# Token blocks 2 and 3 of an adaLN kernel's first part: rows turned by VectorE and a DRAM scratch in place of TensorE transposes

## The chip, the cores and the metric

The kernel runs on one NeuronCore of a Trainium2 chip. The metric is the device time of one execution in microseconds (us). Before the change the median of three runs is 2213.26 us (2213.18 to 2213.31).

A core has five engines with a queue each, and each queue runs in order: TensorE (PE, matmuls and transposes into PSUM), VectorE (DVE), ScalarE (ACT), GpSimd (POOL) and SyncE (SP), which here issues the DMAs. An instruction waits on semaphores at the head of its queue, and all behind it on that engine waits too.

## The reference

One transformer block with adaptive layer norm, on 2048 tokens of width 576, all in float32. Cut to what matters:

```python
mod = (silu(c) @ w_mod).reshape(1, 6, 1, 576)
sa, ca, ga, sb, cb, gb = (mod[:, j] for j in range(6))
h = layernorm(x) * (1 + ca) + sa
x = x + ga * A(h)          # 32 query heads of width 18, one shared key and value head:
                           #   q = h @ wq;  k = h @ wk;  v = h @ wv
                           #   softmax(q k^T / sqrt(18)) v, then @ wo
h = layernorm(x) * (1 + cb) + sb
x = x + gb * B(h)          # layernorm, @ w1 + b1, gelu, @ w2 + b2 (width 4608)
```

The change is in the first lines: from `x` to the transposed, modulated `h` that the projections to q, k and v read.

## The kernel before

The kernel has three parts: projections (to about 129 us), attention, and the channel MLP. Only the first is touched.

The 2048 tokens are four blocks (`tb` 0 to 3) of 512, a block being four tiles (`t`) of 128 tokens. The projections contract over the 576 channels, so `h` is needed with channels on partitions: five chunks (`k` 0 to 4) of 128 channels by 512 tokens, the last with 64 channels held twice. For each block this happens:

- `ln1_stats(tb, t)`: VectorE's bn_stats and bn_aggr and three small GpSimd operations give a tile's scale `rs` and offset `nb`.
- `ln1_apply(tb, t, e)`: the tile is normalised from `XT` into the row buffer `Z1` (L192 on ScalarE, L194 on VectorE): 576 columns, and the last 64 once more.
- `h_chunk(tb, zt, k)`: four 128x128 transposes on TensorE (`tr`, L157) turn a chunk into one PSUM slot of `psB`, of which there are three. Then `h_evac`: ScalarE applies the modulation (L230, into `hf`) and rounds to fp32r (L234, into the buffer `big`), and GpSimd or VectorE takes what the rounding lost (L235).
- `q_chunk(tb, m, zt, mid, n)`: a product. `proj` makes 14 matmuls (L250) into a `psB` slot, ScalarE copies it out twice (L280, L281), GpSimd takes the difference (L282), and SP stores both to the scratch `qscr` in DRAM (L286).

A block has five products, m = 4, 0, 1, 2, 3 at the steps i = 0 to 4 of the loop. In the middle of a product stands a "part": four score matmuls of 512 columns (L321), two for each of the two PSUM slots `psA`, and two VectorE reductions (L346 in `smax_part`) that find the maxima and free the slots.

The order on every engine is the order of the code. The main loop runs over `tb` and the steps, and after the product of a step it places the work for later blocks: chunks of block `tb + 1`, and by the tables `NAPPLY` and `NSTAT` normalisations and statistics of the blocks after. The third and fourth tile of block 2 are normalised at step 0 of block 1 (the first two at step 4 of block 0), those of block 3 at steps 3 and 4 of block 1. The chunks of the next block stand at

```python
for k in {1: (0, 1, 2), 2: (3, 4)}.get(i, ()) if tb else {3: (0, 1, 2), 4: (3, 4)}.get(i, ()):
    h_chunk(tb + 1, nz, k)
```

so in blocks 1 and 2 three chunks follow the product of step 1 and two that of step 2.

Of the kernel before, what the change touches and what calls it, by code (L numbers as in the profile page):

```python
# [8 lines left out]
F32 = mybir.dt.float32  # L9
# [5 lines left out]
S, D, H, DH, F = 2048, 576, 32, 18, 4608  # L15
NB = 4
TB = S // NB
NT = TB // 128
KD = 5
# [13 lines left out]
def block_kernel(ctx: ExitStack, tc, x, wqkv, wo, w1, b1, w2, b2, c, wmod, ident_in, out):  # L33
    nc = tc.nc
    ve, ac, po, pe, sy = nc.vector, nc.scalar, nc.gpsimd, nc.tensor, nc.sync

    per = ctx.enter_context(tc.tile_pool(name="per", bufs=1))
    dr = ctx.enter_context(tc.tile_pool(name="dr", bufs=1, space=bass.MemoryType.DRAM))
# [14 lines left out]
    def psB(): return PS["t"].tile([128, 512], F32, name="psB", bufs=PS["b"])  # L53
# [3 lines left out]
    def big(): return per.tile([128, 10, 512], F32R, name="big", bufs=3)  # L57
# [10 lines left out]
    w2sum = dr.tile([NG, 128, 4, 2, 288], F32, name="w2sum")  # L68
    turned = [dr.tile([D, 128], F32, name="turned%d" % n) for n in range(2)]
    turned0 = dr.tile([D, 128], F32, name="turnedA")  # L70
    qscr = dr.tile([NB, 2, H * DH, TB], F32, name="qscr")


# [15 lines left out]
    p1 = ph1.__enter__()  # L89
# [66 lines left out]
    def tr(o, Z, k):  # L156
        pe.transpose(o, Z[:, 128 * k:128 * (k + 1)], ident)  # L157
# [14 lines left out]
    Zs = {}  # L172
# [3 lines left out]
    def ln1_stats(tb, t):  # L176
        X = XT[:, NT * tb + t, :]
        mv = p1.tile([128, 2], F32, name="mv1", bufs=4)
        rs = p1.tile([128, 1], F32, name="rs1", bufs=12)
        nb = p1.tile([128, 1], F32, name="nb1", bufs=12)  # L180
        ln_stats2(X, ln_stats1(X), mv, rs, nb)
        RN[tb, t] = (rs, nb)

    def ln1_apply(tb, t, e):
        if t == 0:
            Zs[tb] = p1.tile([128, NT, 640], F32, name="Z1")
        Z = Zs[tb]
        X = XT[:, NT * tb + t, :]
        rs, nb = RN.pop((tb, t))
        for o, i in ((Z[:, t, :D], X), (Z[:, t, D:], X[:, 512:])):  # L190
            if e is ac:
                ac.activation(o, i, AF.Identity, scale=rs, bias=nb)  # L192
            else:
                ve.tensor_scalar(o, i, rs, nb, op0=ALU.mult, op1=ALU.add)  # L194

    mcol = p1.tile([128, 2, KD], F32, name="mcol")

# [29 lines left out]
    def h_evac(p, zt, k, e, first=False):  # L227

        hf = p1.tile([128, TB], F32, name="hf", bufs=3)
        ac.activation(hf, p, AF.Identity, scale=mcol[:, 1, k:k + 1], bias=mcol[:, 0, k:k + 1])  # L230
        if first:
            ve.tensor_copy(zt[:, k, :], hf)
        else:
            ac.activation(zt[:, k, :], hf, AF.Copy)  # L234
        e.tensor_tensor(zt[:, KD + k, :], hf, zt[:, k, :].bitcast(F32), op=ALU.subtract)  # L235

    def h_chunk(tb, zt, k):
        p = psB()
        for t in range(NT):
            tr(p[:, 128 * t:128 * (t + 1)], Zs[tb][:, t, :], k)  # L240
        h_evac(p, zt, k, ve if tb == 1 and k in (1, 3, 4) else po, tb == 1 and k < 3)

    def proj(o, wh, wl, c0, c1, zt, mid=None, n=0):
# [28 lines left out]
    def q_chunk(tb, m, zt, mid, n):  # L272

        w = 126 if m < KD - 1 else 128
        wd = 126 if m < KD - 1 else 72
        pq = psB()
        proj(pq[:w], wqh, wql, 126 * m, 126 * m + w, zt, mid, n)
        qs = p1.tile([128, 2, TB], F32R, name="qs", bufs=2)
        qf = p1.tile([128, TB], F32, name="qf", bufs=2)
        ac.activation(qf[:w], pq[:w], AF.Copy)  # L280
        ac.activation(qs[:w, 0], pq[:w], AF.Copy)  # L281
        po.tensor_tensor(qs[:w, 1], qf[:w], qs[:w, 0].bitcast(F32), op=ALU.subtract)  # L282
        if m == KD - 1:
            if tb >= 2:
                key_diff(tb, qf)
        sy.dma_start(qscr[tb, :, 126 * m:126 * m + wd, :].rearrange("s p t -> p s t"), qs[:wd].bitcast(F32))  # L286
        return qf, qs

    def k_block(tb, qs):

        pk = psB()
        for i in range(2):
            pe.matmul(pk, pick[:, i, :], qs[:, i, :], start=(i == 0), stop=(i == 1))
        ac.activation(KS[:, TB * tb:TB * (tb + 1)], pk, AF.Identity, bias=ones)

    def v_block(tb, qf):
        pk = psB()
        for i in range(NT):
            pe.transpose(pk[:, 128 * i:128 * (i + 1)], qf[:, 128 * i:128 * (i + 1)], ident)
        ve.tensor_copy(V[:, NT * tb:NT * (tb + 1), :DH],  # L300
                       pk.rearrange("p (i c) -> p i c", i=NT)[:, :, 72:72 + DH])
# [6 lines left out]
    def load_q(n):  # L308
        tb, qd = divmod(n, NQ)
        if n not in QST:  # L310
            new_q(n)
        q = QST[n]
        for g in range(2):
            for r in range(3):
                src = qscr[tb, r // 2, 4 * DH * qd:4 * DH * (qd + 1), :]
                src = src.rearrange("(p g d) t -> g d p t", p=2, g=2)[g]
                sy.dma_start(q[64 * g + DH * r:64 * g + DH * (r + 1)].bitcast(F32), src)
# [30 lines left out]
    def smax_fin1(n):  # L348
        m = MR[n] = pa.tile([128, 16], F32, name="mxf", bufs=2)
        mm = MX.pop(n)  # L350
        if n == 0:
            ve.tensor_reduce(m, mm, axis=AX.X, op=ALU.max)
        else:
            ve.tensor_reduce(m[:, :8], mm[:, :8, :], axis=AX.X, op=ALU.max)
            ve.tensor_reduce(m[:, 8:], mm[:, 8:, :3], axis=AX.X, op=ALU.max)
# [14 lines left out]
    for t in range(NT):  # L370
        ln1_stats(0, t)
        if t:
            ln1_apply(0, t - 1, ve if t % 2 else ac)
    ln1_apply(0, NT - 1, ac)
    pick = p1.tile([128, 2, 128], F32R, name="pick")
    ones = p1.tile([128, 1], F32, name="ones")
# [28 lines left out]
    def dense(n, w, x):  # L405

        p = psB()
        for _ in range(n):
            pe.matmul(p, w, x, start=True, stop=True)
# [35 lines left out]
    def unit():  # L445
        nonlocal u1
        smax_half(1, u1 % 2, u1 // 2)
        u1 += 1
# [5 lines left out]
    for tb in range(NB):  # L454
        nz = big() if tb + 1 < NB else None
        for i, m in enumerate((4, 0, 1, 2, 3)):
            np_ = NPART[tb][i]
            if i == 2:
                parts.extend((u, tb) for u in range(8))
            mid = {(NB - 1, 1): unit, (NB - 1, 4): lambda: last.popleft()()}.get((tb, i), part)  # L460
            qf, qs = q_chunk(tb, m, zt, mid, np_ + 1 if np_ else 0)
            if i == 0:
                qv = qf, qs
            if i == 1:
                k_block(tb, qv[1])
                v_block(tb, qv[0])
                if tb == 0:
                    load_q(0)
            if i == 2:
                if tb == 0:  # L470
                    load_q(1)
            if tb == NB - 1:
                if i == 0:
                    unit()
                elif i == 3:
                    smax_fin1(0)
                if i == 4:
                    dense(5, wqh[:, 0, :128], KS[:, :512])
                    unit()
                    dense(4, wqh[:, 0, :128], KS[:, :512])  # L480
            if nz is not None:
                for k in {1: (0, 1, 2), 2: (3, 4)}.get(i, ()) if tb else {3: (0, 1, 2), 4: (3, 4)}.get(i, ()):
                    h_chunk(tb + 1, nz, k)
            if tb < 2:
                for _ in range(NAPPLY[tb][i]):
                    b, t = applies.popleft()
                    ln1_apply(b, t, ve if b == 1 and t % 2 else ac)
                for _ in range(NSTAT[tb][i]):
                    ln1_stats(*stats.popleft())
        zt = nz  # L490
# [521 lines left out]
    for n in range(NQT):  # L1012
# [8 lines left out]
        for tok in order:  # L1021
            if tok[0] == "V":
                g = int(tok[1:])
                while g:
                    i = min(g, 4 - pq % 4)
# [16 lines left out]
            elif tok == "WP":  # L1042
                h2 = part.popleft()
                p = psB()
# [495 lines left out]
```

## Time and profile before

| | |
|---|---|
| median of three runs | 2213.26 us |
| the profiled execution's own time | 2214.96 us |
| its span, first to last instruction | 2212.9 us |
| mean granted TensorE clock | 0.998 |
| block 1 of the first part (its products) | about 48.0 to 72.7 us |
| block 2 | about 72.7 to 97.6 us |
| TensorE transposes of the rows of blocks 2 and 3 | 40, at 56.6 to 88.4 us |

Times in the text are microseconds from the span's start. A timeline row has start, length, engine, line, operation, output <- inputs, shape and count, and in brackets how long the engine sat idle before it and what released it. A row that merges several instructions gives the length of the whole group. An engine's next instruction can start before the last one's row ends, since they overlap a little.

### The profile page before, as it was taken

What the parts mean: (1) busy time and instruction counts of PE and PEld (TensorE: products, weight loads), DVE (VectorE), ACT (ScalarE), POOL (GpSimd) and SP (SyncE); (2) the same over time, 40 slices, a digit from 0 to 9 for tenths busy, and PEclk for the clock granted to TensorE, in tenths of its full rate; (3) what the DMA queues carried; (4) which work ended last, traced back from release to release, by engine and by line L of the source; (5) the groups of instructions that cost most, each with busy time, mean ns of one, the idle gap of its engine ahead of it and who ended that gap; (6) DMA issues with size and microseconds to landing.
All of it is one profiled execution on the core that took longest, in us unless ns stands there. A gap on an engine that the chain in (4) does not pass through costs nothing.

```text
span 2212.9 us, 46091 instructions
## 1 busy us (share of the span) xinstructions
PE 2193.5 (99%) x16559; PEld 1441.7 (65%) x16559; DVE 1935.3 (87%) x3421; ACT 1626.0 (73%) x3114; POOL 1520.2 (69%) x1760
## 2 busy tenths in 40 slices
PE   8999999999999999999999999999999999999999
PEld 6654445454544445444454445898988899889898
DVE  7589999999999999999999992888888878787887
ACT  5569999999999999999999998544445444343443
POOL 7654356667777677678675640888899767877776
PEclk9999999999999999999999999999999999999999
DMA  6232143333433443443343321666767746676664
GB/s 228 88 134 93 34 132 119 132 128 114 138 124 128 127 138 103 126 141 117 122 128 124 125 71 59 200 195 190 201 186 202 208 131 179 184 217 189 178 183 124
DMA packets 233528, 317.67 MB, mean 144 GB/s; under 512 B 58351, under 2 KB 124287, under 8 KB 233301
## 3 DMA queue, kind: packets, MB, share of 16 engines
q1 hardware_dynamic: 233157, 314.59, 46.4%
q8 instruction: 131, 2.15, 0.4%
q14 instruction: 96, 0.79, 0.1%
q10 hardware_dynamic: 144, 0.15, 0.0%
HBM read 205.92 MB, written 98.51 MB: 138 GB/s over the span
## 4 chain that ended last, share of the span: by engine, by line
PE 93%; DVE 1%; ACT 1%; issue 0%; ACTq 0%; DVEq 0%
PE psC L952 24%; PE psB L1176 18%; PE psA L1279 16%; PE psB L962 14%; PE psM L321 13%; PE psB L751 2%; PE psB L972 2%; PE psA L1313 1%; PE psA L751 1%; PE psB L250 0%; PE psB L359 0%; PE psM L962 0%; ACT P L964 0%; DVE mx L346 0%; DVE gs L1188 0%; ACT h L1185 0%
## 5 line engine op out<-in xcount | busy, mean ns | idle before, releaser
L964 ACT ACTIVATE P<-psB 128x512 f32<-128x512 f32 x2013 | 1055.6, 621 | 49.0 <-PE psM L321 24.4
L984 DVE TENSOR_REDUCE mx<-psM 128x1 f32<-128x512 f32 x1476 | 930.5, 681 | 27.6 <-PE psM L321 12.9
L962 PE MATMUL psB<-qst,KS 64*128 64x512 f32 x2013 | 604.8, 434 | 0.1
L321 PE MATMUL psM<-KS,qst 64*128 64x512 f32 x1722 | 594.0, 435 | 0.7 <-DVE mx L339 0.3
L952 PE MATMUL psC<-P,V 128*32 128x256 f32 (+3 forms) x6608 | 569.0, 440 | 0.0
L962 PEld LDWEIGHTS psB<-qst,KS 64*128 64x128 f32 x2013 | 302.1, 184 | 215.7 <-ACT P L964 184.6
L321 PEld LDWEIGHTS psM<-KS,qst 64*128 64x128 f32 x1722 | 285.4, 184 | 190.1 <-DVE mx L984 140.9
L1176 PE MATMUL psB<-ops,w1a 128*128 128x512 f32 x1512 | 393.9, 396 | 0.2 <-DVE h L1191 0.2
L1176 PEld LDWEIGHTS psB<-ops,w1a 128*128 128x128 f32 x1512 | 270.1, 188 | 46.8 <-DVE h L1191 0.6
L952 PEld LDWEIGHTS psC<-P,V 128*32 128x32 f32 x6608 | 147.1, 108 | 188.5 <-issue 160.9
L1285 DVE TENSOR_TENSOR XT<-psA,XT 128x576 f32<-128x576 f32 x330 | 241.2, 751 | 16.4 <-PE psA L1279 11.0
L1279 PEld LDWEIGHTS psA<-w2s,big 128*128 128x128 f32 x1584 | 223.6, 188 | 12.1 <-DVE XT L1285 0.2
L1279 PE MATMUL psA<-w2s,big 128*128 128x288 f32 x1584 | 230.1, 294 | 0.0
L1253 POOL TENSOR_TENSOR big<-s,big 128x512 fp32r<-128x512 f32 x132 | 170.9, 1295 | 10.6
L982 DVE CUSTOM_DVE_ANT_0 xc<-psM,xc 128x512 f32<-128x512 f32 x246 | 165.6, 680 | 11.8 <-PE psM L321 4.5
L1185 ACT ACTIVATE h<-psB,b1t 128x512 f32<-128x512 f32 x144 | 97.9, 680 | 105.7 <-PE psB L1176 99.3
L1189 ACT ACTIVATE psB<-gs 128x512 f32<-128x512 f32 x144 | 86.7, 602 | 119.9 <-DVE gs L1188 119.9
L975 ACT ACTIVATE xc<-psB 128x512 f32<-128x512 f32 x246 | 154.3, 627 | 5.5 <-PE psM L321 1.9
L788 POOL TENSOR_TENSOR os<-O,os 128x512 fp32r<-128x512 f32 x31 | 39.8, 1285 | 169.6 <-ACT os L787 169.5
L1188 DVE SCALAR_TENSOR_TENSOR gs<-psB,h 128x512 f32<-128x512 f32 x144 | 98.7, 686 | 38.7 <-ACT psB L1186 38.6
L822 POOL TENSOR_TENSOR r<-r,r 128x256 fp32r<-128x256 f32 (+1 forms) x162 | 121.8, 752 | 13.0
L1194 ACT ACTIVATE big<-h 128x512 fp32r<-128x512 f32 x39 | 24.7, 634 | 139.5 <-DVE h L1191 139.5
(215 smaller groups left out, 3289.2 us busy)
## 6 DMA issues: line engine op xcount, KB each, us to landing
w1a<-w1scr SPq DMA_DIRECT2D x252, 256.0 KB
w2s<-w2sum SPq DMA_DIRECT2D x132, 288.0 KB
w1scr<-r SPq DMA_DIRECT2D x126, 256.0 KB
w2s<-w2scr SPq DMA_DIRECT2D x76, 288.0 KB
w2scr<-r SPq DMA_DIRECT2D x72, 288.0 KB
w2sum<-r SPq DMA_DIRECT2D x72, 288.0 KB
qst<-qscr SPq DMA_DIRECT2D x192, 72.0 KB
w1a<-w2scr SPq DMA_DIRECT2D x33, 288.0 KB
```

The source lines that it names most:

```text
L321: pe.matmul(o, QST[n][64 * g:64 * g + 64, p, 128 * qt:128 * (qt + 1)], KS[64 * g:64 * g + 64, 512 * kb:512 * (kb + 1)], start=True, stop=True)
L822: po.tensor_tensor(o[:, n:2 * n], src, o[:, :n].bitcast(F32), op=ALU.subtract)
L952: pe.matmul(PVt[n][32 * j:32 * (j + 1), cs], V[:, kc, :], t[:, j, cs], start=(kc == 0 and h0 == 0), stop=(kc == 15), skip_group_check=True)
L962: pe.matmul(t, KS[64 * g:64 * g + 64, 128 * kc:128 * (kc + 1)], QST[n][64 * g:64 * g + 64, i, :], start=True, stop=True)
L964: ac.activation(P[n, kc][:, 2 * i + g, :], t, AF.Exp, scale=SCALE)
L975: ac.activation(XC[-1], t, AF.Relu)
L982: ve.tensor_tensor_reduce(c, t, c, 1.0, -3.0e38, ALU.add, ALU.max, o)
L984: ve.tensor_reduce(o, t, axis=AX.X, op=ALU.max)
L1176: pe.matmul(o, x, y, start=(first and i == 0), stop=(i == len(terms) - 1), skip_group_check=True)
L1253: po.tensor_tensor(unit(u, 1), x, unit(u, 0).bitcast(F32), op=ALU.subtract)
L1279: pe.matmul(p[:, i, :288], x[:, ts_], W2S[k][:, y], start=(bool(first) and q == 0), stop=(q == 2), skip_group_check=True)
L1285: ve.tensor_tensor(o, p[:, :, :288], o, op=ALU.add)
```

## The change

For blocks 2 and 3 the rows are no longer turned by TensorE. `ln1_apply` leaves out the second copy of the last 64 columns and lets VectorE transpose the tile in place; that transpose works within squares of 32 by 32. After every second tile SP writes the two tiles to a scratch `hscr` in DRAM (channels by tokens), eight DMAs of 32 partitions by 18 by 32 elements. A new function `h_load` reads the scratch back into the same row buffer, seen as five chunks of 512 tokens. ScalarE then reads a chunk there instead of in PSUM. `Z1` has two buffers instead of one. `h_load` stands at step 1 of the block, and the chunks move from steps 1 and 2 to 2 and 3. Blocks 0 and 1 keep TensorE's transposes.

```diff
+    hscr = [dr.tile([D, TB], F32, name="hscr%d" % n) for n in range(2)]
...
-            Zs[tb] = p1.tile([128, NT, 640], F32, name="Z1")
+            Zs[tb] = p1.tile([128, NT, 640], F32, name="Z1", bufs=2)
...
-        for o, i in ((Z[:, t, :D], X), (Z[:, t, D:], X[:, 512:])):
+        for o, i in ((Z[:, t, :D], X), (Z[:, t, D:], X[:, 512:]))[:1 if tb > 1 else 2]:
...
+        if tb > 1:
+            ve.transpose(Z[:, t, :D], Z[:, t, :D])
+            if t % 2:
+                for p in range(0, 128, 32):
+                    for i in (t - 1, t):
+                        sy.dma_start(hscr[tb % 2][:, 128 * i + p:128 * i + p + 32].rearrange("(c f) n -> f c n", f=32),
+                                     Z[p:p + 32, i, :D].rearrange("f (c n) -> f c n", n=32))
+
+    def h_rows(tb):
+
+        return Zs[tb].rearrange("p t c -> p (t c)").rearrange("p (k n) -> p k n", n=TB)
+
+    def h_load(tb):
+
+        H, scr = h_rows(tb), hscr[tb % 2]
+        sy.dma_start(H[:, :KD - 1], scr[:512].rearrange("(k p) n -> p k n", p=128))
+        for q in range(2):
+            sy.dma_start(H[64 * q:64 * q + 64, KD - 1], scr[512:])
...
     def h_chunk(tb, zt, k):
-        p = psB()
-        for t in range(NT):
-            tr(p[:, 128 * t:128 * (t + 1)], Zs[tb][:, t, :], k)
+        if tb > 1:
+            p = h_rows(tb)[:, k]
+        else:
+            p = psB()
+            for t in range(NT):
+                tr(p[:, 128 * t:128 * (t + 1)], Zs[tb][:, t, :], k)
...
-                for k in {1: (0, 1, 2), 2: (3, 4)}.get(i, ()) if tb else {3: (0, 1, 2), 4: (3, 4)}.get(i, ()):
+                if tb and i == 1:
+                    h_load(tb + 1)
+                for k in {2: (0, 1, 2), 3: (3, 4)}.get(i, ()) if tb else {3: (0, 1, 2), 4: (3, 4)}.get(i, ()):
                     h_chunk(tb + 1, nz, k)
```

How the instructions stand now, on three engines. Line numbers of the changed kernel lie about 20 higher: L249 is the old L230, L302 and L303 the old L280 and L281, L308 the old L286, L368 the old L346.

ScalarE in block 1, before: the key copy of step 1 (`KS`) and behind it the chunks of block 2 (`hf` from a PSUM slot, `big` from `hf`).

```order
L294 ACTIVATE KS_83<-psB_662,ones_194 128x512
L230 ACTIVATE hf_677<-psB_672,mcol_140 128x512
L234 ACTIVATE big_588<-hf_677 128x512
L230 ACTIVATE hf_686<-psB_681,mcol_140 128x512
L234 ACTIVATE big_588<-hf_686 128x512
```

The same place now (`Z1_585` is the row buffer of block 2, `Z1_791` that of block 3).

```order
L316 ACTIVATE KS_85<-psB_680,ones_196 128x512
L302 ACTIVATE qf_727<-psB_703 126x512
L303 ACTIVATE qs_726<-psB_703 126x512
L249 ACTIVATE hf_732<-Z1_585,mcol_142 128x512
L253 ACTIVATE big_598<-hf_732 128x512
```

The first chunk has moved behind the copies of the product of step 2, and reads the loaded row buffer. The normalisations of block 3 (`Z1_791`) follow the fifth chunk, as before.

VectorE across steps 3 and 4 of block 1 in the changed kernel (before, the same rows without the transpose).

```order
L368 TENSOR_REDUCE mx4_610<-psA_762 128x2
L368 TENSOR_REDUCE mx4_610<-psA_766 128x2
L197 STREAM_TRANSPOSE Z1_791<-Z1_791 128x576 x2
L146 BN_STATS bst_807<-XT_74 128x6
L150 BN_STATS bst_807<-XT_74 128x6
L151 BN_AGGR mv1_804<-bst_807 128x2
L368 TENSOR_REDUCE mx4_610<-psA_822 128x2
```

Two transposes of block 3's rows now stand between the reductions of step 3 and those of step 4.

SP's queue from step 3 of block 0 to step 2 of block 1, before: only stores of products to `qscr`.

```order
L286 DMA qscr_71<-qs_491 126x2x512
L286 DMA qscr_71<-qs_559 126x2x512
L286 DMA qscr_71<-qs_613 72x2x512
L286 DMA qscr_71<-qs_656 126x2x512
L286 DMA qscr_71<-qs_732 126x2x512
```

And now.

```order
L308 DMA qscr_73<-qs_493 126x2x512
L308 DMA qscr_73<-qs_561 126x2x512
L201 DMA hscr0_71<-Z1_585 32x18x32 x8
L308 DMA qscr_73<-qs_623 72x2x512
L201 DMA hscr0_71<-Z1_585 32x18x32 x8
L308 DMA qscr_73<-qs_674 126x2x512
L211 DMA Z1_585<-hscr0_71 128x4x512
L213 DMA Z1_585<-hscr0_71 64x512 x2
L308 DMA qscr_73<-qs_726 126x2x512
```

Two groups of eight writes and the load of three DMAs have come in between the stores.

## The prediction

> **What bounds the kernel now.** I read the page first: the busy shares and the chain that ended last.
>
> ```profile
> span 2212.9 us, 46091 instructions
> PE 2193.5 (99%) x16559; PEld 1441.7 (65%) x16559; DVE 1935.3 (87%) x3421; ACT 1626.0 (73%) x3114; POOL 1520.2 (69%) x1760
> PE 93%; DVE 1%; ACT 1%; issue 0%; ACTq 0%; DVEq 0%
> ```
>
> TensorE (PE) is busy 99% of the span and holds 93% of the chain. A microsecond taken from TensorE in its dense stretches is a microsecond of the total, and so is one of new idleness. The change lies in the first 130 us, so next comes the table by stretches, for block 1 (48.0 to 72.7 us) and block 2 (72.7 to 97.6 us). Its columns after the length are the busy times of PE, PEld, DVE, ACT and POOL, the granted clock, the DMA share and GB/s.
>
> ```profile
> 48.00:72.70 24.70, 24.01 (x117) 16.82 (x116) 16.91 (x25) 20.19 (x35) 20.09 (x29) 1.00 0.31 105
> 72.70:97.60 24.90, 23.76 (x115) 16.00 (x113) 12.53 (x12) 14.35 (x25) 13.49 (x11) 1.00 0.28 93
> ```
>
> TensorE binds in both. But in block 1, ScalarE (ACT) is busy 20.2 of 24.7 us and VectorE (DVE) 16.9: an engine that gets new work, or a new wait at the head of its queue, has 5 to 8 us to lose before TensorE feels it.
>
> **What is removed.** The timeline of PE has the transposes (L157) and what stands around them.
>
> ```profile
> 56.57 1.53 PE L157 MATMUL psB<-ident,Z 128*128 128x128 f32 x12 [0.33 <-DVE V L300]
> ...
> 62.30 1.03 PE L157 MATMUL psB<-ident,Z 128*128 128x128 f32 x8
> 63.70 1.90 PE L250 MATMUL psB<-big,wA 128*126 128x512 f32 x7 [0.36 <-ACT qs L281]
> ...
> 73.72 0.73 PE L321 MATMUL psA<-KS,qst 64*128 64x512 f32 x4
> ...
> 87.33 1.04 PE L157 MATMUL psB<-ident,Z 128*128 128x128 f32 x8
> 88.73 1.89 PE L250 MATMUL psB<-big,wA 128*126 128x512 f32 x7 [0.36 <-ACT qs L281]
> ...
> 109.99 1.41 PE L250 MATMUL psB<-big,wA 128*126 128x512 f32 x5 [0.33 <-ACT qs L281]
> ```
>
> In block 1's stretch (rows for block 2) the twelve cost 1.53 us. The eight cost 1.40 (63.70 - 62.30; in block 2's stretch 88.73 - 87.33), their slot wait of 0.36 included: without them the next product takes another of the three psB slots, one long free. The 0.33 ahead of the twelve stays: block 3, which makes no transposes, has it at the same place (109.99). So 2.93 a stretch, **5.9 us** for two, if nothing else comes late.
>
> **What is added, and where it queues.** VectorE gets eight transposes of 128x576, and each pair of tiles is written to DRAM by eight DMAs ("puts") in pieces of 32 floats. No first-part row has these, but the second part makes the same ones. The first row below is VectorE's; the next two are SP's timeline of four puts each; then two stretches with the DMA's share and GB/s last; then the stretch and the SP wait that price a 2 KB-row transfer.
>
> ```profile
> L615 DVE STREAM_TRANSPOSE Z<-Z x8: 767/768/769, 577.6 to 1126.1; 128x576 f32<-128x576 f32 x8
> 1126.88 2.00 SPq L618 DMA_DIRECT2D turnedA<-Z  x4
> 1472.69 2.21 SPq L694 DMA_DIRECT2D turned<-BC  x4
> 1128.00:1130.00 2.00, 2.00 (x16) 0.71 (x16) 1.97 (x7) 1.69 (x5) 1.78 (x3) 1.00 0.73 126
> 1130.00:1132.00 2.00, 2.00 (x17) 0.63 (x17) 1.86 (x5) 2.00 (x5) 1.85 (x3) 1.00 0.02 4
> 35.00:36.00 1.00, 1.00 (x6) 0.79 (x5) 0.97 (x4) 0.96 (x2) 0.33 (x2) 1.00 0.88 285
> SPq L317 <- DMA qscr<-qs: 6.1, 2, 3.3
> ```
>
> A put holds SP for 0.50 to 0.55 us and the DMA engines for 0.58 (73.7 KB at 126 GB/s); the last lands at most 1.1 us after its issue, since the DMA is quiet from 1130. A q store of 516 KB takes 1.8 us at 285 GB/s, yet the next SP instruction waits 3.3 us for its landing, so 1.5 us are fixed.
>
> Now block 2, whose rows are made in block 1. The next rows are ScalarE's and SP's timelines there.
>
> ```profile
> 49.74 2.28 ACT L192 ACTIVATE Z<-XT,nb,rs 128x576 f32<-128x576 f32 x4
> ...
> 62.56 0.60 ACT L280 ACTIVATE qf<-psB 126x512 f32<-126x512 f32 x1 [1.19 <-PE psB L250]
> 63.05 0.59 ACT L281 ACTIVATE qs<-psB 126x512 fp32r<-126x512 f32 x1
> 63.53 0.78 ACT L230 ACTIVATE hf<-psB,mcol 128x512 f32<-128x512 f32 x1
> 64.34 0.64 ACT L234 ACTIVATE big<-hf 128x512 fp32r<-128x512 f32 x1
> 64.88 0.76 ACT L230 ACTIVATE hf<-psB,mcol 128x512 f32<-128x512 f32 x1
> 52.95 0.31 SPq L286 DMA_DIRECT2D qscr<-qs  x1
> ```
>
> 1. *SP.* The rows of tiles 0 and 1 are normalised from 49.74 and turned by 52.2, but their puts stand behind the store of 52.95, free at 53.3. Eight puts at 0.53: 57.5. A store: 57.8. Eight puts of tiles 2 and 3: 62.0. A store: 62.4. Then the load, which waits for the last put.
> 2. *Landing of the puts.* SP alone would give 63.1 (62.0 + 1.1). The DMA engines have from about 53.8 sixteen puts at 0.58 and a 295 KB store (1.0 us): 64.1, and some 0.5 for the landing: **64.6**.
> 3. *The load.* Its first DMA moves 1.05 MB in 2 KB rows: 3.7 us at 285 GB/s, or 2.7 at 389 (a stretch further down), and 1.5 fixed: 4.2 to 5.2. I take 5.0, near the store's rate: **69.6**.
> 4. *ScalarE.* Its first chunk of block 2 now stands behind the copies of block 1's third product (62.56), where before the fourth chunk stood (63.53). Twelve transposes less and the psA waits told below about cancel, so it asks at 63.5 and stands still until 69.6: a new wait of 6.1 us, with everything of ScalarE behind it. A chunk takes 1.35 (64.88 - 63.53), five of them 6.75, the two copies of a product between them 0.97 (63.53 - 62.56): 77.3. Behind them are the first two normalisations of block 3, 0.77 each (a tile's two instructions took 1.14; I take two thirds): 78.9.
> 5. *VectorE.* Block 3's first two transposes wait for these, and behind them in VectorE's queue stand the statistics and the reductions that free TensorE's two psA slots.
>
> ```profile
> 50.49 2.34 DVE L346 TENSOR_REDUCE mx<-psA 128x2 f32<-128x1024 f32 x2
> 52.76 0.44 DVE L145 BATCH_NORM_STATS2 bst<-XT 128x6 f32<-128x288 f32 x1
> ...
> 53.79 2.30 DVE L346 TENSOR_REDUCE mx<-psA 128x2 f32<-128x1024 f32 x2
> ```
>
> The second transpose ends at 79.8, the statistics (1.03, from 52.76 to 53.79) at 80.8, the two reductions (2.36) free their slots at 82.0 and 83.2.
> 6. *TensorE.* The four score matmuls in the first product of block 2 (before: 73.72, done at 74.45) want both slots; they end at about 83.6. That is **9.2 us later**. The idleness begins at some 70 us with short waits for block 2's chunks and is 7 us or more in one piece.
>
> From there block 2 runs densely and its 2.93 is saved: VectorE had only 12.5 us of work in 24.9 there. Block 3's load lands near 98 by the same steps (transposes done at 84.8, puts out by 89, landings and load 7 to 9 more), its last chunk is ready near 107, and TensorE, 6.3 us late, needs it near 107.5. Block 1's transposes are inside the 9.2 already, so the net is 9.2 - 2.9 = **+6.3 us**.
>
> The clock falls in such holes:
>
> ```profile
> 18.00:21.30 3.30, 2.40 (x19) 2.10 (x19) 1.75 (x5) 1.79 (x4) 2.03 (x4) 1.00 1.06 389
> 21.30:24.70 3.40, 3.24 (x8) 2.51 (x8) 3.00 (x6) 3.37 (x6) 0.00 (x0) 0.51 1.07 396
> 24.80:28.20 3.40, 3.39 (x15) 2.42 (x13) 2.94 (x4) 2.67 (x6) 3.17 (x2) 1.00 0.87 317
> 134.00:137.40 3.40, 3.40 (x15) 0.99 (x15) 1.47 (x4) 1.79 (x5) 0.00 (x0) 0.50 1.02 359
> ```
>
> After 3.3 us with 0.9 idle the granted clock is 0.51 for 3.4 us, in which 8 matmuls ran where the next 3.4 us held 15: one such stretch costs half of it, 1.7 us. A hole of 7 us should bring one, at most two: 0 to 3.4, I take **1.7**. The Trainium skill ("TensorE: Matmul & The Clock Gate", Part 1) says the clock halves after an idle window of about 3.4 us and returns after one busy window. The trace agrees with the length (3.4 us at 0.51 and at 0.50), not with the need of a wholly idle window. By the rule the sum is +8.0, by a reading in which this hole goes free +6.3.
>
> The 1 MB load is the other place for a page. The Trainium skill ("DMA: Bandwidth & Descriptors", Measured) gives 6.15 us for 1 MB into SBUF, for another issue path. By that the landing is about 1 us later and the sum +9; the store's rows here give 5.0.
>
> Costed at nothing: the eight small normalisations that go (ScalarE then only waits longer for the load), the second row buffer (block 2's normalisations stand behind block 1's chunks on ScalarE anyway), and VectorE's first four transposes: they hold the reduction of 53.79 back and TensorE by some 1.5 us near 53, but TensorE's arrival no longer sets the end of the hole; if the hole goes, that 1.5 counts. ScalarE reading SBUF rather than PSUM: no row has the same instruction; a copy within SBUF takes 0.64 (64.34), the PSUM read 0.78, the 128x576 one from SBUF scales to at most its own time. Five of them: -0.7 to +0.5, taken as 0.
>
> **Sum.** +9.2 - 2.9 + 1.7 = +8.0. The profiled execution took 2214.96 us with a span of 2212.9, and the runs' median is 2213.26, so it lies 1.7 above them; the sum is a difference and I add it to the median: **2221.3 us**. Bounds: puts landed at 63.1 and the load in 4.2 (2.3 earlier), no clock term: +4.0, 2217.3. Puts and load 1.2 later each and two clock stretches: +12, 2225.5.
>
> **Rivals.**
> - *The load lands in time* (not slower). The point that decides is 63.5 us, when ScalarE asks. Landed by then, every step from 4 on is 6.1 earlier: 9.2 - 6.1 - 2.9 = +0.2, with no hole long enough for the clock: 2213.5. For it: DMA is busy only 0.31 of block 1. Against: SP's sixteen puts alone last until 62.0. Why so little even then: VectorE's transposes still wait behind ScalarE's chunks. Chance 0.16.
> - *The whole 5.9 is kept*: 2207.4. Needs the landing in time and, on top, reductions that are not held by the transposes. VectorE's slack (7.8 us in block 1) speaks for it, its queue order against. Chance 0.06.
> - *Block 3 comes late as well.* If puts and load are 3 us slower than the rows, block 2's hole grows by 3 and block 3's chunks, which I have half a microsecond ahead of need, make one of about 3 with or without a clock term: 2213.3 + 8.0 + 3 + 3 = 2227. Chance 0.12.
> - *Forecast*: 2221.3, chance 0.66.
>
> **Numbers.** About 0.2% (4.4 us) is what can be told from no change. Slower by more: 0.63 of the forecast's 0.66 (its low end lies under +4.4) and 0.12: 0.75. Within: 0.03 and 0.16: 0.19. Faster: 0.06. The range leaves out the 2207 case and the 2227 case: 2212.5 to 2225.5.
>
> **What would show it.** In the profile after: ScalarE idle about 6 us before its first chunk of block 2, released by the DMA from the scratch; VectorE idle some 10 us before the first transpose of block 3, released by ScalarE; TensorE idle 7 us or more before score matmuls early in block 2, released by a reduction; a granted clock near 0.5 for 3.4 us behind it; SP with sixteen puts in 8 to 9 us. I am wrong if the load lands before ScalarE asks, if SP issues puts much faster than 0.5 us, or if block 3's transposes don't hold the reductions.

## The result and the profile after

| | before | after |
|---|---|---|
| median | 2213.31 us (2213.18 to 2214.33, 5 runs) | 2226.65 us (2226.06 to 2227.45, 5 runs) |
| ratio | | 1.006, 95% interval [1.0045, 1.0075] |
| profiled execution, span | 2214.96, 2212.9 us | 2226.65, 2224.6 us |

The changed kernel is 13.3 us slower. The forecast had the sign, but its 2221.3 and its upper end of 2225.5 lie below the time. From span to span the difference is 11.7; the other 1.65 is that the profiled execution of before was 1.65 above its median and that of after on it.

The page of the changed kernel, where the same three lines as before are worth a look:

```profile
span 2224.6 us, 46053 instructions
PE 2194.1 (99%) x16519; PEld 1440.3 (65%) x16519; DVE 1940.3 (87%) x3429; ACT 1623.7 (73%) x3106; POOL 1521.1 (68%) x1760
PE 94%; DVE 3%; ACT 2%; DMA 1%; POOL 1%; issue 1%; SPq 0%; ACTq 0%; POOLq 0%; DVEq 0%
```

TensorE has 40 instructions fewer and is not less busy: what the transposes gave up went into slower matmuls. The span is 11.7 longer, so the rest is idleness, and the chain of waits now runs 3% over VectorE, 2% over ScalarE and 1% over a DMA. The timelines show in which order. First SP: eight puts, a store, eight puts, a store (left out here), the load. Below them are block 3's last eight puts, two stores (the second at 96.88), and block 3's load.

```profile
52.58 4.84 SPq L201 DMA_DIRECT2D hscr<-Z  x8
57.52 0.45 SPq L308 DMA_DIRECT2D qscr<-qs  x1
58.06 4.96 SPq L201 DMA_DIRECT2D hscr<-Z  x8
...
64.76 0.39 SPq L211 DMA_DIRECT2D Z<-hscr  x1
...
86.20 4.83 SPq L201 DMA_DIRECT2D hscr<-Z  x8
91.53 5.66 SPq L308 DMA_DIRECT2D qscr<-qs  x2
97.43 0.38 SPq L211 DMA_DIRECT2D Z<-hscr  x1
```

A put of block 2 takes 0.605 to 0.62 us of SP, and block 2's load goes out at 64.76. Block 3's goes out 6.4 us after its last put: it stands behind the store of the product m=0, and in this stretch SP waits up to 5.0 us for GpSimd's part of a product before it can store it. ScalarE's timeline has the two places where it waits for the scratch, and between them the normalisations of block 3:

```profile
71.42 0.81 ACT L249 ACTIVATE hf<-Z,mcol 128x512 f32<-128x512 f32 x1 [8.63 <-DMA Z<-hscr]
...
79.24 1.61 ACT L193 ACTIVATE Z<-XT,nb,rs 128x576 f32<-128x576 f32 x2
...
105.09 0.82 ACT L249 ACTIVATE hf<-Z,mcol 128x512 f32<-128x512 f32 x1 [4.04 <-DMA Z<-hscr]
```

VectorE's timeline hands the wait on: the transposes of block 3 stand idle for ScalarE, and the reductions that free TensorE's slots stand behind them.

```profile
80.12 1.54 DVE L197 STREAM_TRANSPOSE Z<-Z 128x576 f32<-128x576 f32 x2 [14.06 <-ACT Z L193]
...
82.59 2.30 DVE L368 TENSOR_REDUCE mx<-psA 128x2 f32<-128x1024 f32 x2
```

TensorE's timeline, block 2's first product and, in the last two rows, the same product of block 3:

```profile
72.95 0.49 PE L272 MATMUL psB<-big,wA 128*128 128x512 f32 x1 [3.14 <-ACT big L253]
74.30 3.03 PE L272 MATMUL psB<-big,wA 128*128 128x512 f32 x6 [0.85 <-POOL big L254]
83.82 0.79 PE L343 MATMUL psA<-KS,qst 64*128 64x512 f32 x2 [6.50 <-DVE mx L368]
84.95 0.80 PE L343 MATMUL psA<-KS,qst 64*128 64x512 f32 x2 [0.34 <-DVE mx L368]
85.68 6.09 PE L272 MATMUL psB<-big,wA 128*128 128x512 f32 x14
...
113.24 0.97 PE L272 MATMUL psB<-big,wA 128*128 128x512 f32 x3 [0.45 <-POOL big L254]
114.48 0.50 PE L272 MATMUL psB<-big,wA 128*128 128x512 f32 x1 [0.27 <-POOL big L254]
```

The hole of 6.50 us is where the forecast put it, released by the reduction it named. Before it lies one of 3.14 for block 2's first chunk, and behind it fourteen matmuls take 6.09. The table by stretches, with the granted clock third from the end, shows why:

```profile
70.90:74.30 3.40, 0.50 (x2) 0.19 (x2) 0.00 (x0) 2.82 (x5) 1.27 (x1) 1.00 0.32 122
74.30:77.70 3.40, 3.02 (x6) 1.65 (x6) 0.00 (x0) 3.34 (x6) 3.10 (x4) 0.50 0.00 0
77.70:81.10 3.40, 0.00 (x0) 0.00 (x0) 0.97 (x2) 3.37 (x6) 3.30 (x5) 1.00 0.19 61
81.10:84.50 3.40, 0.68 (x2) 0.29 (x2) 3.30 (x6) 1.93 (x4) 2.45 (x5) 0.50 0.82 184
84.50:87.90 3.40, 3.06 (x9) 2.11 (x8) 3.40 (x5) 0.41 (x1) 0.74 (x1) 0.50 0.83 190
87.90:91.30 3.40, 3.40 (x9) 2.62 (x8) 0.58 (x1) 1.09 (x2) 1.07 (x1) 0.50 1.02 189
```

Three stretches at half clock, 81.10 to 91.30, start inside the hole and run on for 7.5 us behind its end at 83.82; the forecast had one stretch of 3.4. The half clock from 74.30, behind the wait for block 2's first chunk, slows six matmuls (3.03 us) that end 6.5 us before TensorE may go on, so it should cost nothing.

### The profile page after: what moved, and what is told of

Same layout as the page of the kernel before. It is cut to its first block, busy times and chain, and to the rows that moved or that the text cites. A ratio compares the mean times of both kernels' runs of the same rounds, so it can differ in the third digit from the quotient of the medians.

```text
span 2224.6 us, 46053 instructions
## 1 busy us (share of the span) xinstructions
PE 2194.1 (99%) x16519; PEld 1440.3 (65%) x16519; DVE 1940.3 (87%) x3429; ACT 1623.7 (73%) x3106; POOL 1521.1 (68%) x1760
## 4 chain that ended last, share of the span: by engine, by line
PE 94%; DVE 3%; ACT 2%; DMA 1%; POOL 1%; issue 1%; SPq 0%; ACTq 0%; POOLq 0%; DVEq 0%
PE psC L976 24%; PE psB L1200 18%; PE psA L1303 16%; PE psB L986 14%; PE psM L343 13%; PE psB L775 2%; PE psB L996 2%; PE psA L1337 1%; PE psB L272 1%; DMA Z<-hscr 1%; PE psA L775 1%; DVE mx L368 1%; ACT hf L249 0%; PE psB L381 0%; PE psA L343 0%
## 5 line engine op out<-in xcount | busy, mean ns | idle before, releaser
L1006 DVE CUSTOM_DVE_ANT_0 xc<-psM,xc 128x512 f32<-128x512 f32 x246 | 165.6, 680 | 11.7 <-PE psM L343 5.3
```

The source lines that it names most:

```text
L1006: ve.tensor_tensor_reduce(c, t, c, 1.0, -3.0e38, ALU.add, ALU.max, o)
```

## The experiments

Two theories stood at first. The theory that I call the chain: the load lands after ScalarE asks, ScalarE's queue hands the wait to VectorE's transposes, these hold the reductions, TensorE has a hole and then a slow clock. Its rival: the new work itself (transposes, puts, SBUF reads) costs the time wherever it stands. The kernel before ran beside each group: 2213.63 (first four), 2213.67 (e5 to e8), 2213.85 (e9), 2213.58 (e10 and e11).

| run | median us | ratio to before, 95% interval |
|---|---|---|
| e2: no turning at all | 2207.58 | 0.9971 [0.996, 0.9982] |
| e1: turned, no trip through DRAM | 2215.51 | 1.0007 [0.9998, 1.0017] |
| e4: block 3's rows first | 2219.26 | 1.0025 [1.0015, 1.0034] |
| e3: load ahead of a store | 2223.85 | 1.0044 [1.0027, 1.006] |
| e5: hole filled with matmuls | 2224.32 | 1.0047 [1.0034, 1.006] |
| e8: e4 and e3 together | 2217.77 | 1.0019 [1.001, 1.0028] |
| e6: block 3 alone | 2213.29 | 0.9998 [0.9989, 1.0006] |
| e7: block 3 alone, load first | 2211.22 | 0.9989 [0.998, 0.9998] |
| e9: half the puts on GpSimd | 2251.99 | 1.0172 [1.0154, 1.019] |
| e10: half the puts on ScalarE | 2226.77 | 1.0058 [1.0043, 1.0073] |
| e11: e8 and e10 together | 2224.45 | 1.0049 [1.0033, 1.0066] |

### e2 and e1: the saving, the turning and the trip

e2 leaves out VectorE's transposes, the puts and the load; e1 keeps the transposes and leaves out puts and load. In both, ScalarE reads untransposed rows of the right size in SBUF, so what q, k and v are made from is not the reference's for blocks 2 and 3.

```diff
# e1 and e2
-            p = h_rows(tb)[:, k]
+            p = Zs[tb][:, k % NT, :TB]
...
-                if tb and i == 1:
-                    h_load(tb + 1)
...
-                        sy.dma_start(hscr[tb % 2][:, 128 * i + p:128 * i + p + 32].rearrange("(c f) n -> f c n", f=32),
-                                     Z[p:p + 32, i, :D].rearrange("f (c n) -> f c n", n=32))
# e2 alone
-            ve.transpose(Z[:, t, :D], Z[:, t, :D])
```

> Neither the transposes on VectorE nor the way through DRAM: only TensorE's 40 transposes are taken out and the chunks stand a step later; the output is not the reference's. Theory T: the full 5.9 us come, 2207 us (2206 to 2209). Rival (the chunks' later place costs by itself): 2211 us or more.

> VectorE's transposes stay, the way through DRAM (writes and load) is left out, and ScalarE reads the row buffer as it is, so the output is not the reference's. Theory T (the time is lost because the load lands long after ScalarE asks for it, and ScalarE's standstill is handed on to VectorE's transposes and from them to TensorE): the hole goes, and what is left is the transposes' hold on the reductions, which eats the gain: 2211 to 2215 us. Rival Q (the eight transposes in VectorE's queue are themselves the cost): at least half of the 13.3 us stays, 2219 us or more.

e2 took 2207.58, so the 5.9 us of removed transposes are real: 6.05 below before. e1 took 2215.51, just above the 2211 to 2215 expected, and the hole did not go. Turning on VectorE alone thus costs 7.9 and eats the whole gain, although ScalarE has its rows at once in that run. VectorE's and TensorE's timelines of e1:

```profile
71.66 1.53 DVE L197 STREAM_TRANSPOSE Z<-Z 128x576 f32<-128x576 f32 x2 [5.35 <-ACT Z L193]
```

```profile
75.36 0.79 PE L338 MATMUL psA<-KS,qst 64*128 64x512 f32 x2 [3.68 <-DVE mx L363]
```

Even without a late load, VectorE waits 5.35 us for ScalarE to come through its five chunks to block 3's normalisations, and TensorE has a hole of 3.68, behind which its fourteen matmuls take 5.71 (77.21). In e2, where the reductions have nothing ahead of them that waits, the same place in TensorE's timeline has no wait and the full clock:

```profile
69.99 0.73 PE L336 MATMUL psA<-KS,qst 64*128 64x512 f32 x4
70.66 3.52 PE L265 MATMUL psB<-big,wA 128*128 128x512 f32 x14
```

From e1 to the changed kernel, 11.1 us, is the trip through DRAM. The loss is therefore about 6 gained, 8 lost to the turning, by its place in the queues, and 11 to the trip.

### e4: the rows of block 3 ahead of block 2's chunks

```diff
-    NSTAT = ((2, 2, 2, 2, 0), (1, 1, 1, 1, 0))
-    NAPPLY = ((0, 2, 2, 0, 2), (2, 0, 0, 2, 2))
+    NSTAT = ((2, 2, 2, 2, 0), (2, 2, 0, 0, 0))
+    NAPPLY = ((0, 2, 2, 0, 2), (2, 0, 4, 0, 0))
...
+            if tb == 1:
+                rows()
             if nz is not None:
```

(`rows` is the loop over NAPPLY and NSTAT, which in block 0 stays where it was.)

> Block 3's statistics, normalisations and transposes are placed ahead of block 2's chunks (statistics at steps 0 and 1, the four tiles at step 2, before the chunks), so VectorE's transposes no longer wait behind ScalarE's standstill; load and chunks stay where they are. Theory T: the reductions are free, the hole at the score matmuls goes, and TensorE waits only for the chunks themselves: 5 to 8 us less than after, 2218 to 2222 us, with half-clock time under 7 us. Rival (the standstill reaches TensorE by another way, through the chunks alone): 2225 us or more.

2219.26, 7.4 below the changed kernel. VectorE and TensorE:

```profile
64.12 3.05 DVE L197 STREAM_TRANSPOSE Z<-Z 128x576 f32<-128x576 f32 x4
67.10 4.58 DVE L368 TENSOR_REDUCE mx<-psA 128x2 f32<-128x1024 f32 x4
```

```profile
73.77 0.50 PE L272 MATMUL psB<-big,wA 128*128 128x512 f32 x1 [1.97 <-ACT big L253]
75.11 0.97 PE L272 MATMUL psB<-big,wA 128*128 128x512 f32 x3 [0.84 <-POOL big L254]
```

The transposes run without a wait, the slots are free before block 2's score matmuls want them, and the hole there is gone, although the load still lands at 72.2. What is left is the direct wait for the chunks and the clock behind it: the fourteen matmuls that follow (79.23) still take 5.16. So the link over VectorE's queue is shown by an edit that touches only the order, of ScalarE's, GpSimd's and VectorE's work for block 3's rows.

### e3: the load ahead of a store

The load was queued behind the 516 KB store of product m=0. Here it goes ahead of it.

```diff
+        if m == 0 and tb in (1, 2):
+            h_load(tb + 1)
         sy.dma_start(qscr[tb, :, 126 * m:126 * m + wd, :].rearrange("s p t -> p s t"), qs[:wd].bitcast(F32))
...
-                if tb and i == 1:
-                    h_load(tb + 1)
```

> Only the order on SP: the load of the turned rows is issued ahead of the store of the product m = 0, no longer behind it. Theory T with the DMA queue as the place of the missing 1.8 us: the load lands some 1.5 to 2.5 us sooner for block 2 and for block 3, so 2222 to 2225 us (after: 2226.65). Rival (the load is slow in itself, whatever stands ahead of it): 2226 us or more.

2223.85, as expected in time; the landing moved less. SP's two loads and ScalarE's first chunk of block 2:

```profile
65.65 0.38 SPq L211 DMA_DIRECT2D Z<-hscr  x1
...
92.90 0.38 SPq L211 DMA_DIRECT2D Z<-hscr  x1
```

```profile
71.58 0.81 ACT L249 ACTIVATE hf<-Z,mcol 128x512 f32<-128x512 f32 x1 [7.87 <-DMA Z<-hscr]
```

Only 0.76 of the 1.5 to 2.5 comes off ScalarE's wait (7.87 against 8.63). More comes from block 3, whose load goes out at 92.90 instead of 97.43 and is there before ScalarE asks: its wait of 4.04 is gone, and TensorE goes from the first to the second group of score matmuls of that product in 2.49 us (110.89 to 113.38), where the changed kernel took 3.75 (111.17 to 114.92). From issue to use block 2's load took 5.9 us here and 6.7 behind the store.

### e5: does the low clock cost anything?

```diff
+    FILL = 26
...
+            dense(FILL, wqh[:, 0, :128], KS[:, :512])
```

(Once, ahead of block 2's first score matmuls.)

> The changed kernel with 26 matmuls of 512 columns, whose results nobody reads, put ahead of block 2's first score matmuls, so that TensorE works through the 6.5 us in which it stood idle there and its clock has no reason to fall. Theory (the half clock behind the hole is a price of its own, about 2.6 us for the 14 matmuls that took 6.1 instead of 3.5): no stretch at half clock behind the hole, those 14 matmuls back at about 3.5 us, and 2223 to 2225, about 2224. Rival (the lower clock only fills time in which TensorE would wait for its operands anyway): 2226 to 2228, with waits after the score matmuls in place of the slow matmuls.

```profile
77.84 6.51 PE L438 MATMUL psB<-KS,wA 128*128 128x512 f32 x26
84.56 0.50 PE L343 MATMUL psA<-KS,qst 64*128 64x512 f32 x2 [0.21 <-DVE mx L375]
85.69 0.50 PE L343 MATMUL psA<-KS,qst 64*128 64x512 f32 x2 [0.63 <-DVE mx L375]
86.12 3.52 PE L272 MATMUL psB<-big,wA 128*128 128x512 f32 x14
```

The hole is filled to 0.21, the fourteen matmuls are back at 3.52, and the time is 2224.32: 2.3 less with 26 matmuls more. The clock is a price of its own, 2.3 us here.

### e9 and e10: is the load late for SP's issues or for the DMA engines?

```diff
-                        sy.dma_start(hscr[tb % 2][:, 128 * i + p:128 * i + p + 32].rearrange("(c f) n -> f c n", f=32),
+                        (po if i % 2 else sy).dma_start(hscr[tb % 2][:, 128 * i + p:128 * i + p + 32].rearrange("(c f) n -> f c n", f=32),
```

(e9; e10 has `ac` for `po`.)

> The changed kernel with the puts of every second tile issued by GpSimd instead of SP; nothing else. Theory A (the load waits for SP, which issues sixteen puts one after the other at about 0.6 us): each queue has eight, block 2's load is issued 3 to 5 us sooner (60 to 62 instead of 64.8) and lands as much sooner, ScalarE's wait falls from 8.6 to 4 to 6 us, and the time is 2220 to 2224. Theory B (the sixteen DMA engines, busy 0.8 to 1.0 of that stretch with the puts' 128-byte pieces, set the landing): SP is free sooner but the load is issued less than 1.5 us sooner, since it waits for the last put to land, and the time is 2225 to 2228.

> The changed kernel with the puts of every second tile issued by ScalarE instead of SP. GpSimd's puts went out one in 2.5 us, so that run could not tell the queue from the DMA engines; ScalarE had an idle 3 us in each of the two places where the puts stand in block 1, and the before-kernel's ScalarE issues DMAs elsewhere. Theory A (the load waits for SP's sixteen issues at 0.6 us): each queue has eight, block 2's load is issued 3 to 4 us sooner than 64.8 and lands as much sooner, ScalarE's wait falls from 8.6 to 4.5 to 6 us, time 2221 to 2224. Theory B (the sixteen DMA engines, busy 0.8 to 1.0 with the puts' 128-byte pieces, set the landing): SP is done sooner but the load, which waits for the last put, is issued less than 1.5 us sooner, ScalarE's wait stays above 7 us, time 2225 to 2229.

e9 missed both theories, at 2251.99: GpSimd sends one put per 2.46 us, and TensorE waits for GpSimd's other work behind them. GpSimd's timeline:

```profile
57.63 0.69 POOL L201 DMA_DIRECT2D hscr<-Z  x1 [3.69 <-issue]
60.11 0.67 POOL L201 DMA_DIRECT2D hscr<-Z  x1 [1.80 <-issue]
62.56 0.67 POOL L201 DMA_DIRECT2D hscr<-Z  x1 [1.78 <-issue]
```

That run says nothing on the question. e10 does, in SP's timeline and in one row of ScalarE's queue:

```profile
53.36 3.69 SPq L201 DMA_DIRECT2D hscr<-Z  x4
...
58.44 4.28 SPq L201 DMA_DIRECT2D hscr<-Z  x4
...
64.61 0.38 SPq L211 DMA_DIRECT2D Z<-hscr  x1
```

```profile
52.21 2.79 ACTq L201 DMA_DIRECT2D hscr<-Z  x4
```

SP has half the puts, but its first four take 0.92 us each instead of 0.605. From ScalarE's first to SP's fourth (52.21 to 57.05) the eight take 4.84, as long as SP's eight alone did; the second eight take 4.28 (from 58.44) against 4.96. The load goes out at 64.61 instead of 64.76, which is 0.9 sooner when each profile is counted from the score matmuls at the head of block 1 (48.66 here, 47.87 in the changed kernel). The two queues share one limit; from 53 to 61 us the DMA engines are busy 0.90 to 1.10. The Trainium skill ("DMA: Bandwidth & Descriptors", Issuing engines are not separate DMA queues) says that the same sixteen engines serve all issuers, and that a second issuer saves only issue time; this run agrees, with the 4.84 unchanged. Theory B holds for the issue of the load; its "wait stays above 7 us" missed (3.10), since ScalarE itself came later: its copies stood 3.27 behind its own puts, TensorE lost 3.38 at 61.88, and the total stayed at 2226.77.

### e6 and e7: block 3 alone

```diff
-        if tb > 1:
+        if tb > 2:
...
-                if tb and i == 1:
+                if tb == 2 and i == 1:
                     h_load(tb + 1)
-                for k in {2: (0, 1, 2), 3: (3, 4)}.get(i, ()) if tb else {3: (0, 1, 2), 4: (3, 4)}.get(i, ()):
+                for k in ({3: (0, 1, 2), 4: (3, 4)}, {1: (0, 1, 2), 2: (3, 4)}, {2: (0, 1, 2), 3: (3, 4)})[tb].get(i, ()):
```

(In e6 `tb > 1` becomes `tb > 2` at three places. e7 moves the load as in e3.)

> Only block 3's rows go by VectorE and DRAM; block 2 keeps TensorE's transposes and its chunks at steps 1 and 2 of block 1. Theory (block 2's hole comes from its load being asked for before it can land; block 3's rows have block 2's spare VectorE time): no wait of ScalarE in block 1, no hole at block 2's score matmuls, 1.5 us of transposes less in block 2's stretch. If block 3's load, issued at step 1 of block 2, lands before ScalarE asks for it: 2210 to 2212. If it is asked for first, as in the changed kernel (there 4.0 us of waiting and about 1.3 us lost in block 3): 2211.5 to 2214. Rival (the turning on VectorE and its puts cost the time, wherever they stand): half the changed kernel's loss, about 2220.

> The kernel with only block 3 turned by VectorE and DRAM, and its load issued ahead of the store of block 2's product m=0. Theory: the load lands before ScalarE asks (no wait on it in block 2's stretch), and the 1.5 us of the transposes that are gone remain: 2210.5 to 2212.5, under the kernel before (about 2213.5) by 1 to 3. Rival (VectorE's transposes in block 1 hold its reductions and with them TensorE, whatever the load does): 2213.5 or more, with a new wait of score matmuls on a reduction.

e6 took 2213.29, far from the 2220 of the rival by which the new work costs the time wherever it stands: no hole in block 2, but the load late in block 3. TensorE there:

```profile
100.61 0.96 PE L272 MATMUL psB<-big,wA 128*128 128x512 f32 x3 [1.00 <-POOL big L254]
101.85 0.50 PE L272 MATMUL psB<-big,wA 128*128 128x512 f32 x1 [0.28 <-POOL big L254]
```

e7 took 2211.22, and its TensorE timeline keeps only one of the two waits:

```profile
100.75 0.50 PE L272 MATMUL psB<-big,wA 128*128 128x512 f32 x1 [0.18 <-POOL big L254]
```

The time came as expected, the wait did not: ScalarE still stands 3.23 us before its chunk at 91.35 (5.23 in e6, at 92.48). It can afford to: the chunk that comes last holds TensorE for 0.18 only. e7 beats the changed kernel by 15.4 us and the kernel before by 2.4, with an interval that just excludes no change; that is less than the 0.2% that the prediction took as what can be told.

### e8 and e11: both blocks, with the repairs together

e8 is e4 with the load as in e3; e11 adds e10's edit.

> The changed kernel with both blocks turned, block 3's statistics, normalisations and transposes ahead of block 2's chunks, and both loads ahead of the store of product m=0. Theory: the two gains add (the load first took 2.8 us off the changed kernel, the rows first 7.4, of which some is the same wait): 2215.5 to 2218.5, no wait of ScalarE for block 3's load, one of about 5 us for block 2's. Rival (what is left after the rows come first isn't the load's landing): 2219 to 2221, no change against the kernel with the rows first alone.

> The kernel with block 3's rows ahead of block 2's chunks and both loads ahead of the store of product m=0, with, on top, the puts of every second tile on ScalarE's queue. Theory A: block 2's load 3 to 4 us sooner and no store held behind sixteen puts: 2212 to 2216 against 2217.8 without the second queue. Theory B: the DMA engines are the limit, and ScalarE's issues stand ahead of its copies: 2217 to 2221.

e8 took 2217.77, 1.5 below e4 (their two intervals overlap), with the waits that were expected (4.88 for block 2's load, none for block 3's). Part of what is left is new, in ScalarE's timeline:

```profile
71.44 0.82 ACT L249 ACTIVATE hf<-Z,mcol 128x512 f32<-128x512 f32 x1 [4.88 <-DMA Z<-hscr]
...
86.99 0.60 ACT L303 ACTIVATE qs<-psB 128x512 fp32r<-128x512 f32 x1 [4.56 <-DMA qscr<-qs]
```

Block 3's sixteen puts now stand in one piece on SP (15.0 us from 68.3), the stores of block 2 stand behind them, and a copy waits for its buffer. e11 takes this away, and is slower, 2224.45, above what either theory gave: ScalarE's own puts hold its copies, and TensorE has holes of 4.38 at 62.87 and 3.75 at 78.07. No version with both blocks came down to the kernel before.

## Why the prediction was too low

The chain that makes block 2's hole was right: e1, e3 and e4 each took away or shortened one link, e5 the clock behind it, and each time the median moved the way the chain asks. Three terms had the wrong size, and for block 3 the path was wrong.

Two profiles can be compared only from a common mark, since they differ before the change has any part in it. The score matmuls at the head of block 1, before and after:

```profile
48.67 0.73 PE L321 MATMUL psA<-KS,qst 64*128 64x512 f32 x4
```

```profile
47.87 0.74 PE L343 MATMUL psA<-KS,qst 64*128 64x512 f32 x4
```

The profile of after has them 0.8 earlier; e3 and e5, with the same code up to there, have them at 48.82 and 48.68. So a time that the forecast counted in the first profile compares with a time of the second plus 0.8 ("by the mark" below).

- **Steps 1 and 2, SP and the landing of the puts: 1.0 too early.** The load was expected at 64.6 and went out at 64.76, which is 1.0 late by the mark: puts took 0.605 to 0.62 instead of 0.53, sixteen times. That the two figures agree is luck. e10 shows that the DMA engines set the pace of the puts more than SP does; the forecast had both and took the engines.
- **Step 3, the load: the largest error.** It was taken at 5.0 us and took 6.66 (64.76 to 71.42). With step 2 the landing is 2.6 late by the mark. Without the store just ahead it took 5.9 to 6.1 (e3, e7, e8), so the store ahead accounts for some 0.7. For the other 0.9 to 1.1 the traces give two candidates. The forecast priced the first of the load's three DMAs alone, and the other two carry 0.26 MB more, 0.9 us at its 285 GB/s. And the start is slow: in e3 the engines moved 36 GB/s in the first 2.35 us from the issue and 378 GB/s in the 3.58 up to the first use, where 1.5 were taken as fixed. No run separates them. The Trainium skill's figure ("DMA: Bandwidth & Descriptors", Measured), 6.15 for 1 MB on another issue path, was nearer than the rate taken from the store's row.
- **Steps 4 to 6: right, and late by what steps 2 and 3 missed.** The score matmuls end at 85.75 (84.95 + 0.80). By the mark that is 12.1 later than before instead of 9.2, so 2.9 too late, and 2.6 of it is the landing.
- **The transposes: right.** 6.05 by e2, for 5.9.
- **The clock: mis-sized.** One stretch was taken, 1.7, because the holes before the change bring one. Here three follow one another and reach 7.5 us past the hole; e5 puts the price at 2.3 (the fourteen matmuls alone, by their rows, at 2.6: 6.09 against 3.52). The bound of 3.4 held.
- **Block 3 at nothing: wrong, and by another path.** Its load was to follow the puts and land near 98. The puts were out at 91.03, but the load stood in SP's queue behind the store of block 2's product m=0, which went out at 96.88, and landed at 105.1. TensorE's 3.75 us between the groups of score matmuls were 2.49 before (100.30 to 102.79): 1.3 lost. e3, which moves the load ahead of that store, took this loss away by the place alone.

Sum by these rows: 12.1 - 3.0 + 2.6 + 1.3 = 13.0, against 13.3 between the medians, 12.5 between the spans from the mark on (11.7 + 0.8), and 8.0 forecast. What is left over, half a microsecond at most, was not traced further.

Of the rivals, "block 3 comes late as well" gave 2227, and the time is 2226.65. Its condition, puts and load 3 us slower, was nearly met, with 2.6, and block 2's hole grew by about that. But its 3 us in block 3 were 1.3, and came from SP's queue; the clock made up 0.9 of the difference. That the number is so close is partly luck. "The load lands in time" was priced at 2213.5; e1 measured that case, without the puts, at 2215.51. It held that no hole would be long enough for the clock, and a hole of 3.68 was. "The whole 5.9 is kept" needed the reductions not to be held by the transposes: e2, which leaves the transposes out, has that, at 2207.58 against the 2207.4 given.

The bounds were too narrow because the high end moved the puts, the load and the clock but left block 3 at nothing.

## What to carry to other kernels

When TensorE work is moved to another engine, price first what that engine's queue has waiting behind the new instruction: here the turning cost 7.9 us by its place among reductions (e1), more than the 6 it freed, and in the changed kernel, moving block 3's statistics, normalisations and transposes a few places ahead gave 7.4 back (e4). A round trip through DRAM needs a lead of its puts, their landing and the load together (19 us here, 52.6 to 71.4). Here it paid only for block 3, whose first tiles are normalised 19 us before ScalarE asks for their chunks (69.2 to 88.1 in e7); block 2's have 14 (49.0 to 62.8). A DMA also waits for whatever its queue holds ahead of it, so look at what each store in that queue waits for. If one late event feeds several terms of a sum, let the range move them together. And when two profiles are compared, find a mark ahead of the change first.

## What the runs showed of the hardware

- **The clock stayed low through busy stretches.** The Trainium skill ("TensorE: Matmul & The Clock Gate", Part 1) has the full clock return after one busy window of about 3.4 us. The stretch from 84.50 has TensorE busy for 3.06 of 3.40, and the next is still at 0.50; yet after 74.30, busy for 3.02, the clock is back at 1.00. Lengths and the fall after an idle stretch agree with the page, and busy time alone doesn't tell which stretch brings the clock back. What does was not tried.
- **The price of a hole varies.** The same fourteen matmuls, 3.52 us at the full clock, took 6.09 behind the changed kernel's hole of 6.50, 5.63 in e3 behind one of 6.48, 4.78 in e9 behind one of 6.48, and 5.71 in e1 behind one of only 3.68.
- **GpSimd sends a put every 2.46 us** (e9), SP one in 0.58 to 0.62 (the changed kernel), for the same 72 KB in pieces of 32 floats.
- **A second hardware queue brought little for such pieces**: with ScalarE and SP issuing side by side, eight puts took 4.84 and 4.28 us in place of SP's 4.84 and 4.96 (e10).
- **The load took 5.9 to 8.7 us from issue to first use**, and what stood just ahead of it in SP's queue divides the runs: without a store there 5.9 to 6.1 (block 2 in e3 and e8, block 3 in e7), with one 6.6 to 8.7 (6.66 and 7.66 in the changed kernel, 8.42 in e6, 8.65 for block 3 in e4, 89.99 to 98.64). By what path the store slows the load was not tried.
